# Sample 0's first chunk stores scores for two later chunks, and GpSimd splits its values

## The chip, the cores and the metric

The kernel runs on one core of a Trainium2 chip. The metric is the device time in microseconds (us) of one execution; smaller is better. TensorE multiplies matrices, VectorE and ScalarE work element by element, GpSimd does the same and issues some of the transfers, and SyncE issues transfers only. In the profile they are called PE (with PEld for its weight loads), DVE, ACT, POOL and SP. Each engine takes its own instructions strictly in the order in which they were written; semaphores hold an instruction back until its inputs are there.

## What is computed

Three layers run one after the other on two samples of 3136 tokens with 256 features. The first is an attention without softmax:

```python
scores = scale * np.matmul(z, z.transpose(0, 2, 1))   # scale = 1 / 3136, z is 64 wide
attn = np.maximum(scores, 0.0) ** 2
out = np.matmul(attn, v)
return (u * out).astype(np.float32)
```

Behind it come a mixing layer of rank 32 with a two-layer network of width 1024, and a Fourier mixing layer with normalization and a second network of that width. Only the attention is touched here. Its scores are symmetric: the score of token i against token j is the score of j against i.

## The kernel before

**The attention.** For each sample b the 3136 tokens are taken as queries in seven chunks of 448 (`qc` 0 to 6, `NC` = 7, `CH` = 448). Against one chunk the keys go in 13 steps: twelve pairs of 128 keys (`p` 0 to 11) and a last half pair (`p` = 12). A step has two parts. In `scores`, PE does six matmuls of 448 columns on half of its rows each, so that two run side by side; ACT applies the relu (L735) and the square (L736); then the result is split into a high part `h` (a rounded copy) and a low part `l` (the subtraction, L136). The copy is done by DVE (L742) or, for a "swift" step, by ACT (L133). In `values`, PE multiplies the values `Vt`, which are split in the same way, with `h` and `l`: 24 matmuls for a full pair (L769). Scores are made two steps ahead of the values that use them (`LAG` = 2).

**Kept scores.** Because of the symmetry a step may read its scores instead of making them. In a chunk, `_stored` names the parts of a step's scores that a later chunk will need. For such a step, which the planner calls heavy, `keep` has DVE transpose the scores 32 by 32 into a `turned` tile (L684), and transfers of 112 KB, issued by POOL and SP by turns (L691), write them to `kept_d`. In the later chunk `load_kept` fetches 448 KB through ACT's queue three steps ahead (L665), and `split_kept` makes `h` on ACT and `l` on DVE. No matmul is done, and no relu or square. In sample 0, chunk 0 keeps nothing, so pairs 0 and 1 are always made anew; chunk 4 reads 5 of its 13 steps and chunk 5 reads 6. In sample 1 the same chunks read 7 and 8.

**Order.** `_pairs` sets the order of the 13 steps. Read steps go to fixed places, the half pair to place 6, and the made ones fill the rest, bare ones (nothing to store) first. `ahead(i)` writes out what belongs to step i: the split of the values if this is sample 0's first chunk, the scores, a load of kept scores, the stores of the step before, and pieces of other work: key and query loads, and conversions of weights with their own loads.

**The first chunk.** Chunk 0 of sample 0 also prepares all values of its sample: for each pair a load of 256 KB, a copy to the high part on ACT (L133) and a subtraction for the low part on DVE (L136), both in `parts_v`. The loads go through a few buffers (`vraw`, `stg`, two of each), so SP can issue one only when an older one has been split. POOL has no arithmetic in this chunk: it issues half of the key loads and the next query load, and near the chunk's end it loads constants and makes an identity matrix.

Of the kernel before, what the change touches and what calls it, by code (L numbers as in the profile page):

```python
# [15 lines left out]
ALU = mybir.AluOpType  # L16
# [5 lines left out]
CH = 448  # L22
NC = S // CH
# [20 lines left out]
def _plain(b, p):  # L44
    return (b == 0) & (p < 2)


def _kept(b, qc):

    return [p for p in range(12) if 256 * (p + 1) <= qc * CH and (b or 256 * p >= CH)]  # L50


def _target(p, a):
    return (4 * p + a) // 7, (4 * p + a) % 7 * 64


def _stored(b, qc, p):

    if qc == NC - 1 or not (b or qc):
        return []  # L60
    if p == 12:
        return [(a, NC - 1, 384 + 32 * a) for a in range(2)]
    return [(a, *_target(p, a)) for a in range(4) if _target(p, a)[0] > qc]
# [54 lines left out]
def f(ap):  # L118
    return ap.bitcast(F32)
# [3 lines left out]
def program(ctx, tc, zT, v, uT, U, V, w1a, w2a, w1b, w2b, b49, f64, fd, rep, mask, out):  # L123
    nc = tc.nc
# [7 lines left out]
    def hcopy(o, i):  # L132
        nc.scalar.copy(o, i)  # L133

    def sub(o, a, b):
        tt(out=o, in0=a, in1=b, op=ALU.subtract)  # L136
# [6 lines left out]
    def ctile(tag, dt=F32, **k):  # L143
        return com.tile([128, 2 * CH], dt, tag=tag, name=tag, **k)

    def ptile():
        return ctile("P", bufs=4)

    def c2(t):
        return t.rearrange("p (a n) -> p a n", a=2)  # L150

    def run(gen):
        for _ in gen:
            pass
# [7 lines left out]
    kept_d = {  # L162
        (b, c): dram.tile([c * CH, CH], F32, tag=f"kept{b}{c}", name=f"kept{b}{c}")
        for b in range(NB)
        for c in range(1, NC)
        if _kept(b, c)
    }
    V_d = dram.tile([2 * RANK, S], F32R, tag="Vd", name="Vd")
# [313 lines left out]
    def attention(stack):  # L482
# [11 lines left out]
        def turned_tile():  # L494
            return att.tile([128, 2 * CH], F32, tag="turned", name="turned", bufs=5)
# [97 lines left out]
        def split_v(b, p):  # L593
            run(parts_v(b, p))

        def parts_v(b, p):
            raw, n = vraw.pop((b, p)), 2 if p < 12 else 1
            t = Vt[b, p] = big.tile([128, 2, 2, D], F32R, tag=f"V{p}", name=f"Vt{p}", bufs=1)
            hcopy(t[:, 0:n, 0, :], raw[:, 0:n, :])
            yield  # L600
            sub(t[:, 0:n, 1, :], raw[:, 0:n, :], f(t[:, 0:n, 0, :]))


        def stage():
# [55 lines left out]
        def load_kept(b, qc, p):  # L660
            own = next((k for k in range(2) if loads[k] not in kept), None)
            A = kept[b, qc, p] = ptile() if own is None else turned_tile()
            if own is not None:
                loads[own] = b, qc, p
            nc.scalar.dma_start(out=c2(A), in_=kept_d[b, qc][256 * p : 256 * p + 256].rearrange("(m j) n -> m j n", j=2))  # L665

        def split_kept(b, qc, p):
            A, h, l = kept.pop((b, qc, p)), ctile("h", F32R), ctile("l", F32R)
# [29 lines left out]
        def scores(b, qc, p):  # L698
            ps = psS.tile([128, 2, 512], F32, tag="S", name="psS")
            extra = psO.tile([128, 512], F32, tag="O11", name="psO11") if (b, qc, p) == (0, 0, 0) else None  # L700
            q = Q[b, qc]

            w = CH if p < 12 else CH // 2
            for kk, kq in ((0, 0), (0, 1), (1, 0)):
                for j, r in enumerate(halves):
                    if p == 12:
                        k = KTl[b][r, kk]
                    elif (b, qc) == (0, 0) and p < 2:
                        c = 256 * p + 128 * j
                        k = q[r, kk, c : c + 128]  # L710
                    else:
                        k = KT[b][r, p, kk]
                    o = j * w if p == 12 else 0
                    if extra is None:
                        mm(ps[:, j, 0:w], k, q[r, kq, o : o + w], start=(kk, kq) == (0, 0), stop=kk == 1)  # L715
                    elif (kk, kq) == (0, 0):
                        dst = extra if j else ps[:, j]
                        mm(dst[:, 0:w], first_q[r, c : c + 128], first_q[r, 0:w], start=True, stop=True)
            A, h, l = ptile(), ctile("h", F32R), ctile("l", F32R)

            if (b, qc, p) == (0, 0, 0):
                x, y, B = slice(0, w), slice(w, 2 * w), ptile()
                act(out=A[:, x], in_=ps[:, 0, 0:w], func=AF.Relu, scale=1.0 / S)
                nc.vector.tensor_scalar(
                    out=B[:, y], in0=extra[:, 0:w], scalar1=1.0 / S, scalar2=0.0, op0=ALU.mult, op1=ALU.max
                )
                run(first_v)
                for k, m in ((x, A), (y, B)):
                    act(out=m[:, k], in_=m[:, k], func=AF.Square)
                    nc.vector.tensor_copy(h[:, k], m[:, k])  # L730
                for k, m in ((x, A), (y, B)):
                    sub(l[:, k], m[:, k], f(h[:, k]))
            else:
                x = slice(0, 2 * w)
                act(out=A[:, x].rearrange("p (a n) -> p a n", a=2), in_=ps[:, :, 0:w], func=AF.Relu, scale=1.0 / S)  # L735
                act(out=A[:, x], in_=A[:, x], func=AF.Square)  # L736
                stored = _stored(b, qc, p)
                heavy[0] += bool(stored)
                if turns:
                    keep()  # L740
                swift = stored and heavy[0] % 3 and p != pairs_of[b, qc][-1]
                (hcopy if swift else nc.vector.tensor_copy)(h[:, x], A[:, x])  # L742
                r = slice(0 if p < 12 else 64, 128)
                sub(l[r, x], A[r, x], f(h[r, x]))
                if stored:
                    turns.append((b, qc, p, A))
            prob[b, qc, p] = (h, l)

        acc, heavy = {}, [0]
# [130 lines left out]
        pairs_of = {(b, qc): _pairs(b, qc) for b in range(NB) for qc in range(NC)}  # L880
        order, last_order = pairs_of[0, 0], pairs_of[0, NC - 1]
# [11 lines left out]
        t = att.tile([128, 5, D], F32R, tag="an", name="warm", bufs=1).rearrange("p a n -> p (a n)")  # L893
# [7 lines left out]
        for k in range(20):  # L901
            r, n = halves[k % 2], 128 if k < 8 else 352
# [4 lines left out]
        first_q = qraw[0, 0]  # L907
        split_q(0, 0)
        first_v = parts_v(0, 0)
        next(first_v)  # L910
        split_z(0, 0, slice(2, 3))
        scores(0, 0, 0)

        def ahead(i):
            if i < len(steps):
# [9 lines left out]
                if i + 3 < len(steps) and steps[i + 3][2] in _kept(*steps[i + 3][0:2]):  # L925
                    load_kept(*steps[i + 3])
# [32 lines left out]
        for i in range(-LAG, len(steps)):  # L959
# [3 lines left out]
            if i >= 0:  # L963
                b, qc, p = steps[i]
# [8 lines left out]
                n = i % NP  # L973
# [9 lines left out]
                if (b, qc) == (1, NC - 1):  # L983
                    if n == 2:
                        chunks[0].load()
                        a = c2(turned_tile())
# [316 lines left out]
    with tc.manual_schedule():  # L1303
# [23 lines left out]
        for i in range(nstep + 2):  # L1327
# [3 lines left out]
            early = kp == 7 and i > 2 and chunks[cp].layer == 2  # L1331
# [21 lines left out]
            if i in fetches:  # L1353
                b, k0, k1 = fetches[i]
# [57 lines left out]
```

## Time and profile before

| quantity | value |
|---|---|
| median of 3 runs | 1098.09 us (1093.29 to 1099.11) |
| the profiled execution's own time | 1097.44 us |
| its span, first to last instruction | 1095.7 us |
| PE busy | 1082.7 us, 99% of the span |
| DVE busy | 849.0 us, 77% |
| ACT busy | 622.3 us, 57% |
| POOL busy | 238.0 us, 22% |
| mean granted clock of PE | 0.997 of full speed |

Matmuls are pipelined and their ends are modelled, so PE's busy share says that it seldom stood still, not that it was at its peak. The places where it did stand still are found in the time line, by gaps in front of its instructions. The attention takes the first 513 us, in fourteen chunks of 32 to 39 us each; their borders can be read from the `gate` of each chunk (L801), which is the first work on a chunk's finished sums. A stretch from gate to gate is one chunk's pace.

### The profile page before, as it was taken

How to read it: one execution, taken by the hardware profiler on the slowest of the kernel's cores; microseconds unless marked ns; L12 is line 12 of the kernel's file. 1: busy time of each engine (PE TensorE's matmuls, PEld its weight loads, DVE VectorE, ACT ScalarE, POOL GpSimd, SP SyncE). 2: the span in 40 equal slices, each digit the busy share in tenths (PEclk: the TensorE clock that was granted, in tenths of full speed). 3: DMA queues.
4: the chain of work that ended last, by engine and by line, in shares of the span. 5: the costliest groups of instructions: out<-in, count | busy, mean ns of one | idle time of the engine just before them, and what ended most of it. 6: DMA issues, size and time to landing. Idle time of an engine off the chain costs nothing.

```text
span 1095.7 us, 21312 instructions
## 1 busy us (share of the span) xinstructions
PE 1082.7 (99%) x7926; PEld 1010.2 (92%) x7926; DVE 849.0 (77%) x1571; ACT 622.3 (57%) x1094; POOL 238.0 (22%) x394
## 2 busy tenths in 40 slices
PE   9999999989999999999999999999999999999998
PEld 8999999979999999899899999999999999999997
DVE  7898888778999988666667777676688888778863
ACT  7888777747898777553334444334345454445431
POOL 2143332110534232121111121111141111011110
PEclk9999999999999999999999999999999999999999
DMA  6366668674767677985813454221153231121210
GB/s 176 94 168 169 178 175 239 188 240 131 202 186 197 202 214 214 287 239 156 244 45 112 123 177 110 73 78 44 44 130 110 71 89 46 35 60 51 59 43 34
DMA packets 182248, 148.81 MB, mean 136 GB/s; under 512 B 115734, under 2 KB 156474, under 8 KB 182144
## 3 DMA queue, kind: packets, MB, share of 16 engines
q1 hardware_dynamic: 152416, 77.84, 26.4%
q0 software_dynamic: 21296, 43.21, 14.1%
q10 hardware_dynamic: 8432, 26.40, 8.0%
q8 instruction: 62, 1.02, 0.4%
q14 instruction: 42, 0.34, 0.1%
HBM read 88.61 MB, written 58.75 MB: 134 GB/s over the span
## 4 chain that ended last, share of the span: by engine, by line
PE 79%; DVE 7%; DMA 6%; ACT 4%; issue 2%; SPq 0%; POOL 0%; DVEq 0%; ACTq 0%
PE psO L769 24%; PE psH L427 8%; PE psH L429 8%; PE psC L454 8%; PE psH L428 8%; PE psC L452 8%; PE psC L453 8%; PE psS L715 4%; DVE l L136 2%; DMA kept<-turned 2%; DVE turned L684 1%; ACT P L736 1%; ACT P L735 1%; DMA stg<-in_v 1%; ACT h L133 1%
## 5 line engine op out<-in xcount | busy, mean ns | idle before, releaser
L769 PE MATMUL psO<-h,Vt 64*128 64x448 f32 x2744 | 335.2, 362 | 4.5 <-DVE h L742 3.9
L769 PEld LDWEIGHTS psO<-h,Vt 64*128 64x128 f32 x2744 | 279.5, 185 | 21.4 <-DVE h L742 7.3
L432 ACT ACTIVATE Hh<-psH 128x448 fp32r<-128x448 f32 x224 | 121.5, 543 | 244.2 <-PE psH L429 240.6
L433 DVE SCALAR_TENSOR_TENSOR Hl<-psH,Hh 128x448 fp32r<-128x448 f32 x224 | 138.0, 618 | 109.3 <-ACT Hh L432 107.3
L136 DVE TENSOR_TENSOR l<-P,h 128x896 fp32r<-128x896 f32 (+2 forms) x185 | 167.2, 911 | 57.7 <-ACT h L133 50.2
L769 PE MATMUL psO<-l,Vt 64*128 64x448 f32 x1372 | 194.8, 362 | 3.2 <-DVE l L136 3.0
L427 PE MATMUL psH<-h,w 128*128 128x448 f32 x448 | 164.9, 368 | 0.0
L429 PE MATMUL psH<-h,w 128*128 128x448 f32 x448 | 162.4, 363 | 0.0
L454 PE MATMUL psC<-Hh,w 128*128 128x448 f32 x448 | 162.4, 362 | 0.0
L428 PE MATMUL psH<-l,w 128*128 128x448 f32 x448 | 162.2, 362 | 0.0
L453 PE MATMUL psC<-Hl,w 128*128 128x448 f32 x448 | 162.1, 362 | 0.0
L452 PE MATMUL psC<-Hh,w 128*128 128x448 f32 x448 | 162.0, 362 | 0.0
L769 PEld LDWEIGHTS psO<-l,Vt 64*128 64x128 f32 x1372 | 148.4, 185 | 13.1 <-DVE l L136 7.3
L691 POOL DMA_DIRECT2D kept<-turned x134 | 87.4, 656 | 176.9 <-DVE turned L684 142.4
L735 ACT ACTIVATE P<-psS 128x896 f32<-128x896 f32 (+1 forms) x124 | 107.9, 871 | 28.6 <-PE psS L715 25.2
L736 ACT ACTIVATE P<-P 128x896 f32<-128x896 f32 (+1 forms) x124 | 113.1, 912 | 3.9
L133 ACT CAST h<-P 128x448 fp32r<-128x448 f32 (+1 forms) x108 | 77.0, 724 | 55.0 <-DVE P L318 39.6
L427 PEld LDWEIGHTS psH<-h,w 128*128 128x128 f32 x448 | 84.1, 188 | 6.3 <-issue 0.3
L453 PEld LDWEIGHTS psC<-Hl,w 128*128 128x128 f32 x448 | 84.0, 187 | 6.0
L428 PEld LDWEIGHTS psH<-l,w 128*128 128x128 f32 x448 | 84.2, 188 | 5.8
L715 PE MATMUL psS<-Q,KT 64*128 64x448 f32 x654 | 89.3, 362 | 0.0
L452 PEld LDWEIGHTS psC<-Hh,w 128*128 128x128 f32 x448 | 83.9, 187 | 5.7 <-issue 0.2
(299 smaller groups left out, 1379.8 us busy)
## 6 DMA issues: line engine op xcount, KB each, us to landing
turned<-kept ACTq DMA_DIRECT2D x52, 448.0 KB, 4.1
kept<-turned POOLq DMA_DIRECT2D x123, 112.0 KB, 3.7
kept<-turned SPq DMA_DIRECT2D x118, 112.0 KB, 3.7
uT<-in_uT SPq DMA_DIRECT2D x14, 448.0 KB, 4.4
out<-P SPq DMA_DIRECT2D x27, 224.0 KB, 1.9
aTd<-turned POOLq DMA_DIRECT2D x13, 448.0 KB, 5.9
scr<-wst SPq DMA_DIRECT2D x16, 256.0 KB, 2.0
vraw<-in_v SPq DMA_DIRECT2D x13, 256.0 KB, 4.8
```

Source lines behind the costliest of these rows:

```text
L136: tt(out=o, in0=a, in1=b, op=ALU.subtract)
L427: mm(ps[:, 0:CH], wh, self.h[:, a], start=a == 0, stop=False)
L428: mm(ps[:, 0:CH], wh, self.l[:, a], start=False, stop=False)
L429: mm(ps[:, 0:CH], wl, self.h[:, a], start=False, stop=a == 1)
L432: act(out=h, in_=ps[:, 0:CH], func=AF.Relu)
L433: stt(out=l, in0=ps[:, 0:CH], scalar=0.0, in1=f(h), op0=ALU.max, op1=ALU.subtract)
L452: mm(dst, wh, h, start=k == 0, stop=False)
L453: mm(dst, wh, l, start=False, stop=False)
L454: mm(dst, wl, h, start=False, stop=k == 7)
L715: mm(ps[:, j, 0:w], k, q[r, kq, o : o + w], start=(kk, kq) == (0, 0), stop=kk == 1)
L736: act(out=A[:, x], in_=A[:, x], func=AF.Square)
L769: mm(o[fa][i][:, 0:CH], vt[r, j, k, fa * 128 : fa * 128 + 128], x[r, j * CH : j * CH + CH], start=n0 == 0 and fa not in [t[1][0] for t in ...
```

## The change

Three things are changed. First, `_kept` lets chunks 4 and 5 of sample 0 read pairs 0 and 1 as well, and `_stored` has chunk 0 store what they need: four quarters each of pairs 7, 8 and 9 and two of pair 10. The pairs 0 and 1 of sample 0 lie in another layout of keys, so `load_kept` reads those in two blocks. Second, in `parts_v` GpSimd makes both parts of the values in sample 0, except for the first pair. Third, of the four steps of chunk 0 that now store, those of pairs 7 and 9 have their `h` made by ACT; the counter `heavy`, which chooses swift steps later on, leaves chunk 0 out.

```diff
 def _kept(b, qc):
-    return [p for p in range(12) if 256 * (p + 1) <= qc * CH and (b or 256 * p >= CH)]
+    return [p for p in range(12) if 256 * (p + 1) <= qc * CH and (b or 256 * p >= CH or qc in (4, 5))]
...
-    if qc == NC - 1 or not (b or qc):
+    if qc == NC - 1:
         return []
+    if not (b or qc):
+        return [(a, *_target(p, a)) for a in range(4) if p < 12 and _target(p, a)[0] in (4, 5)]
...
             t = Vt[b, p] = big.tile([128, 2, 2, D], F32R, tag=f"V{p}", name=f"Vt{p}", bufs=1)
-            hcopy(t[:, 0:n, 0, :], raw[:, 0:n, :])
-            yield
-            sub(t[:, 0:n, 1, :], raw[:, 0:n, :], f(t[:, 0:n, 0, :]))
+            early = b == 0 and p != order[0]
+            (nc.gpsimd.tensor_copy if early else hcopy)(t[:, 0:n, 0, :], raw[:, 0:n, :])
+            yield
+            (nc.gpsimd if early else nc.vector).tensor_tensor(
+                out=t[:, 0:n, 1, :], in0=raw[:, 0:n, :], in1=f(t[:, 0:n, 0, :]), op=ALU.subtract
+            )
...
-            nc.scalar.dma_start(out=c2(A), in_=kept_d[b, qc][256 * p : 256 * p + 256].rearrange("(m j) n -> m j n", j=2))
+            how = "(j m) n -> m j n" if _plain(b, p) else "(m j) n -> m j n"
+            nc.scalar.dma_start(out=c2(A), in_=kept_d[b, qc][256 * p : 256 * p + 256].rearrange(how, j=2))
...
                 stored = _stored(b, qc, p)
-                heavy[0] += bool(stored)
+                heavy[0] += bool(stored) and b + qc > 0
                 if turns:
                     keep()
-                swift = stored and heavy[0] % 3 and p != pairs_of[b, qc][-1]
+                swift = stored and (heavy[0] % 3 if b + qc else p % 2) and p != pairs_of[b, qc][-1]
```

What this does to the order is seen at three places. A row has the line, the operation, the tile written and the tiles read, its shape, and how often it comes in a row; numbers behind a name tell buffers apart. The lines of the changed file stand a few higher than in the file before.

The first place is POOL's queue in chunk 0 of sample 0, behind the load of the first keys. Before:

```order
L512 DMA turned_181<-in_zT 64x64
L510 DMA turned_224<-in_zT 64x768
L510 DMA turned_324<-in_zT 64x768
L565 DMA qraw_331<-in_zT 64x448 x2
L508 DMA turned_418<-in_zT 64x2x128 x2
masks.py:197 MEMSET ident_90 128x128
```

And now:

```order
L514 DMA turned_181<-in_zT 64x64
L602 CAST Vt1_186<-vraw_149 128x2x256
L604 ISA
L604 TENSOR_TENSOR Vt1_186<-vraw_149,Vt1_186 128x2x256
L602 CAST Vt2_207<-vraw_154 128x2x256
L604 TENSOR_TENSOR Vt2_207<-vraw_154,Vt2_207 128x2x256
L512 DMA turned_224<-in_zT 64x768
L602 CAST Vt3_287<-stg_184 128x2x256
L604 TENSOR_TENSOR Vt3_287<-stg_184,Vt3_287 128x2x256
L602 CAST Vt4_307<-stg_205 128x2x256
L604 TENSOR_TENSOR Vt4_307<-stg_205,Vt4_307 128x2x256
L512 DMA turned_324<-in_zT 64x768
```

The splits of the values stand in front of the key loads that POOL issued one after the other before.

The second place is DVE's queue around the ninth and tenth steps of chunk 0 (pairs 7 and 8). Before:

```order
L136 TENSOR_TENSOR Vt7_492<-stg_375,Vt7_492 128x2x256
L742 CAST h_503<-P_502 128x896
L136 TENSOR_TENSOR l_504<-P_502,h_503 128x896
L136 TENSOR_TENSOR KT_0_161<-turned_418,KT_0_161 128x2x128
L136 TENSOR_TENSOR Q_515<-qraw_331,Q_515 128x448
L136 TENSOR_TENSOR Vt8_524<-vraw_423,Vt8_524 128x2x256
L742 CAST h_535<-P_534 128x896
L136 TENSOR_TENSOR l_536<-P_534,h_535 128x896
```

And now:

```order
L138 TENSOR_TENSOR l_504<-P_502,h_503 128x896
L138 TENSOR_TENSOR KT_0_161<-turned_418,KT_0_161 128x2x128
L138 TENSOR_TENSOR Q_515<-qraw_331,Q_515 128x448
L690 STREAM_TRANSPOSE turned_539<-P_502 128x14x2x32
L748 CAST h_535<-P_534 128x896
L138 TENSOR_TENSOR l_536<-P_534,h_535 128x896
L690 STREAM_TRANSPOSE turned_584<-P_534 128x14x2x32
L138 TENSOR_TENSOR l_581<-P_579,h_580 128x896
```

The subtractions for the values are gone from DVE, and a transpose stands in front of the next step's `h`.

The third place is ACT's queue at the start of chunk 5 of sample 0, behind the gate's copies from `psO`. Before:

```order
L133 COPY turned_3021<-psO10_2510 128x448
L735 ACTIVATE P_3035<-psS_3028 128x896
L736 ACTIVATE P_3035<-P_3035 128x896
L133 CAST KT_1_2771<-vraw_2883 128x2x128
L735 ACTIVATE P_3051<-psS_3044 128x896
L736 ACTIVATE P_3051<-P_3051 128x896
L665 DMA turned_3058<-kept05_79 128x896
L216 ACTIVATE stg_2829<-stg_2829,maskc_92 128x256
L217 ACTIVATE stg_2829<-stg_2829,maskc_92 128x256
L133 CAST h_3099<-turned_2964 128x896
```

And now:

```order
L135 CAST h_3054<-turned_2925 128x896
L671 DMA turned_3058<-kept05_79 128x896
L218 ACTIVATE stg_2835<-stg_2835,maskc_92 128x256
L219 ACTIVATE stg_2835<-stg_2835,maskc_92 128x256
L135 CAST h_3099<-turned_2972 128x896
L135 CAST KT_1_2777<-vraw_2978 128x2x128
L135 CAST h_3140<-P_3050 128x896
L671 DMA turned_3144<-kept05_79 128x896
L135 CAST w_2953<-stg_2835 128x2x128
L135 CAST h_3178<-turned_3058 128x896
```

Four read steps (`h_3054`, `h_3099`, `h_3140`, `h_3178`) now follow one another, with the weights' copy `w` between the third and the fourth; before, made steps stood between the read ones.

## Rows read from the trace of the kernel before

**Rows 1.** The page: busy time by engine, and the chain that ended last.
```profile
PE 1082.7 (99%) x7926; PEld 1010.2 (92%) x7926; DVE 849.0 (77%) x1571; ACT 622.3 (57%) x1094; POOL 238.0 (22%) x394
PE 79%; DVE 7%; DMA 6%; ACT 4%; issue 2%; SPq 0%; POOL 0%; DVEq 0%; ACTq 0%
```
**Rows 2.** Windows from gate to gate: sample 0's chunks 0, 4, 5, 6; sample 1's 4, 5.
```profile
core 0: us, PE busy (x) PEld busy (x) DVE busy (x) ACT busy (x) POOL busy (x), PEclk, DMA share, GB/s
8.08:43.83 35.75, 35.49 (x354) 32.35 (x354) 31.91 (x49) 31.38 (x46) 4.51 (x8) 1.00 0.46 125
...
153.60:189.78 36.18, 35.53 (x357) 34.61 (x355) 29.90 (x49) 28.07 (x42) 11.39 (x18) 1.00 0.82 230
189.78:224.98 35.20, 33.92 (x332) 30.78 (x330) 29.12 (x49) 24.25 (x38) 5.97 (x9) 1.00 0.66 183
224.98:263.70 38.72, 35.66 (x325) 33.04 (x323) 26.58 (x36) 22.42 (x32) 3.25 (x5) 0.91 0.70 213
...
411.34:443.76 32.42, 32.17 (x325) 30.81 (x323) 26.65 (x38) 22.63 (x31) 8.29 (x13) 1.00 0.80 225
443.76:477.73 33.97, 33.72 (x347) 30.90 (x345) 21.91 (x26) 18.78 (x23) 5.93 (x9) 1.00 0.86 254
```
**Rows 3.** Chain of waits in chunk 0: start, length, what; one step.
```profile
23.31 0.60 PE psS L715 x6
23.91 2.40 PE psO L769 x24
```
**Rows 4.** Groups by form in chunk 0 (8.08 to 43.83 us): busy, mean ns, idle before.
```profile
L136 DVE TENSOR_TENSOR l<-P,h 128x896 fp32r<-128x896 f32 x12 | 13.1, 1092 | 1.1
...
L742 DVE CAST h<-P 128x896 fp32r<-128x896 f32 x12 | 7.5, 623 | 2.6 <-ACT P L736 2.5
L136 DVE TENSOR_TENSOR Vt<-stg,Vt 128x512 fp32r<-128x512 f32 x6 | 4.1, 684 | 0.0
L133 ACT CAST Vt<-stg 128x512 fp32r<-128x512 f32 x6 | 3.7, 609 | 0.0
...
L136 DVE TENSOR_TENSOR KT<-turned,KT 128x384 fp32r<-128x384 f32 x3 | 1.7, 553 | 0.0
...
L136 DVE TENSOR_TENSOR Q<-qraw,Q 128x448 fp32r<-128x448 f32 x1 | 0.6, 619 | 0.0
```
**Rows 5.** Groups by form on DVE, 0 to 270 us: the transpose of a stored step.
```profile
L684 DVE STREAM_TRANSPOSE turned<-P 128x896 f32<-128x896 f32 x28 | 30.8, 1100 | 0.2
```
**Rows 6.** Groups by form on POOL, whole span: a write of 512 columns, a transfer's issue.
```profile
L691 POOL DMA_DIRECT2D kept<-turned x134 | 87.4, 656 | 176.9 <-DVE turned L684 142.4 <-DVE turned L681 23.6 <-DVE stg L214 3.6
...
L1063 POOL MEMSET nh<- 32x512 f32 x3 | 1.6, 519 | 0.0
```
**Rows 7.** Time lines of POOL and DVE where both work: start, length, instruction.
```profile
8.94 0.69 POOL masks.py:199 TENSOR_SCALAR_AFFINE_SELECT ident<-ident 128x128 f32<-128x128 f32 x1
...
9.39 0.78 DVE L136 TENSOR_TENSOR Vt<-vraw,Vt 128x512 fp32r<-128x512 f32 x1
...
529.39 0.28 DVE L214 TENSOR_SCALAR Tl<-Tl 128x256 int32<-128x256 int32 x1
...
548.17 0.67 POOL L1063 MEMSET nl<- 32x512 f32 x1
...
548.29 0.69 DVE L214 TENSOR_SCALAR Tl<-Tl 128x256 int32<-128x256 int32 x1
```
**Rows 8.** ACT in chunk 5 by form: a read step's copy, the weights' copy.
```profile
L133 ACT CAST h<-turned 128x896 fp32r<-128x896 f32 x6 | 5.6, 931 | 0.0
...
L133 ACT CAST w<-stg 128x256 fp32r<-128x256 f32 x3 | 1.2, 407 | 6.8 <-DMA stg<-in_w1a 3.9 <-DVE stg L221 2.9
```
**Rows 9.** Chunk 6 of sample 0: PE's time line, then the window around its gap.
```profile
244.02 1.11 PE L769 MATMUL psO<-h,Vt 64*128 64x448 f32 x3 [3.03 <-DVE h L742]
...
240.00:250.00 10.00, 6.97 (x41) 6.08 (x41) 6.32 (x9) 6.82 (x11) 0.00 (x0) 0.67 0.75 236
```

## Prediction

> **What bounds the kernel now.** I read the page first: PE is busy 99% of the span and carries 79% of the chain that ended last [rows 1]. So work taken from PE is time won, and work put on other engines costs only where PE comes to wait for it. Next I cut the attention from gate to gate [rows 2]. A made step costs PE 0.60 us of scores and every full step 2.40 us of values [rows 3], so a chunk with k read steps cannot be shorter than 12 x 2.40 + 0.60 for the half pair's values, plus 12 x 0.60 + 0.30 for its scores, minus 0.60 k: 36.9 - 0.6 k. Chunk 4 (k = 5) should take 33.9 and takes 36.18; chunk 5 (k = 6) should take 33.3 and takes 35.20; chunk 6 (k = 8) should take 32.1 and takes 38.72 [rows 2]. Chunk 0 shows no such loss: PE is busy for 35.49 of 35.75 us, with DVE at 31.91 and ACT at 31.38 beside it [rows 2]. The reader is to see two things there: in chunk 0 PE sets the pace already, and DVE and ACT stand only 3.8 and 4.4 us below it.
>
> **What the change removes.** Four scoring steps, two in chunk 4 and two in chunk 5. On PE that is 4 x 0.60 = 2.4 us [rows 3]; 24 score matmuls less stand in PE's order. This lies on the path. On DVE a step that is read spares one conversion, 0.62 us [rows 4], and on ACT two passes for one copy of 0.93 us [rows 8]; both engines are below the pace in these chunks (29.90 and 28.07 of 36.18 us [rows 2]), so I count this at nothing, except that it may soften the chunks' short waits, by less than 1 us. In chunk 0, 11 full and one half split of the values leave DVE (11.5 x 0.684 = 7.9 us) and ACT (11.5 x 0.609 = 7.0 us) [rows 4]. Since PE did not wait there, this wins nothing by itself.
>
> **What it adds in chunk 0.** Four transposes on DVE, 4 x 1.10 = 4.4 us [rows 5]. Two conversions go from DVE to ACT (1.2 us off DVE). DVE's own sum thus falls by 7.9 + 1.2 - 4.4 = 4.7 us. Fourteen writes of 112 KB fall on transfer engines that are busy 0.46 of this stretch [rows 2]: hidden. Their issue costs POOL 7 x 0.656 = 4.6 us [rows 6].
>
> POOL gets the splits. No row shows GpSimd copying or subtracting such a tile. The nearest is a write of 512 columns without any input, 0.519 us [rows 6]; a copy should not be cheaper. DVE's subtraction of this size takes 0.684 us [rows 4], so 0.52 + 0.68 = 1.2 us is the low end for a split. The high end comes from the one POOL operation that reads: 0.69 us for 128 columns [rows 7]; four times that, 2.76 us, and 0.52 give 3.3 us. I take the sub at two passes of the memset, one for each input, 1.04 us, and the split at 1.56 us, because the memset has the right number of columns while the 0.69 us includes a wait, as I argue next. So 11.5 x 1.56 = 18 us of arithmetic, beside about 15 transfers at 0.656 = 10 us, in a stretch of 35.75: POOL is not the bound by its own sum. The Trainium skill ("GPSIMD Engine Reference", Performance versus the Vector engine) gives 4497 ns for an add of 2048 columns; a quarter is 1.12 us (an estimate), and with it the split would be 1.64 us and the sum below 0.9 us longer.
>
> **The collision.** The rows show POOL and DVE holding each other up. DVE's L214 takes 0.28 us alone and 0.69 us when a POOL memset runs beside it; it ends where the memset ends [rows 7]. At 9.39 us a DVE subtraction of 512 columns takes 0.78 us against a mean of 0.684 [rows 4, 7], in the only place where POOL was reading SBUF, and that POOL operation needed 0.69 us for 128 columns. I read this as one resource that one of the two holds for a whole instruction. That a conversion collides is firm; that a subtraction with two inputs does rests on one event of 0.1 us. The Trainium skill ("SBUF — State Buffer", Who interferes with whom) states it for both: a conversion in the two-port mode collides with any GpSimd operation, a DVE instruction with two inputs in SBUF with one that reads. By that rule, the trace agrees; its page "Perfetto Trace Analysis" warns that moving work between these two may not help for this reason.
>
> If both collide, their times add up. DVE keeps in chunk 0: 11 subtractions x 1.092 = 12.0, nine conversions x 0.623 = 5.6, key and query subtractions 1.7 + 0.6 = 2.3; together 19.9 us [rows 4]. The transposes have one input; I let POOL run beside them. POOL's 18 us make it 37.9 us. All this has to happen between PE's first values and the last values' start, some 33 us of the 35.75. So chunk 0 grows by **5 us**. With a split of 1.2 us the same sum gives 33.7 and +1; with 3.3 us POOL alone needs 38 + 10 = 48 us and chunk 0 grows by 15. Without any collision it grows by nothing.
>
> POOL's order adds a smaller risk: the key loads L512 and the constants now stand behind splits, and ACT's copy of the keys, then its relu, queue behind a late key load. With the split at 1.56 the loads still come in time; this is in the high end.
>
> **What it adds in chunks 4 and 5.** Four loads of 448 KB, 1.8 MB. Sample 1's chunks 4 and 5 already read seven and eight steps with the same places and take 32.42 and 33.97 us [rows 2], 0.3 below and 1.9 above the bound, though with transfers at 0.80 and 0.86. Sample 0 has keys of the next sample and weights to load besides. In chunk 5 ACT already stood for 3.9 us at the weights' copy for its transfer [rows 8]; this cost PE little, because made steps followed. Now four read steps follow one another there and that copy stands in front of the fourth. Each read step needs 448 KB within 2.4 us, 187 KB per us, near the 183 to 254 GB/s that these chunks reach in all [rows 2]. I price lateness there at +1 us, between -1 (the waits soften) and +6 (below).
>
> **Sum.** Against the profiled execution's own 1097.4 us (0.65 below the median, which I do not correct for): -2.4 + 5 + 1 = +3.6, that is **1101.0 us**.
>
> **The rivals.**
> - *No collision of subtractions, POOL hidden.* Then chunk 0 stays as it is and the four steps are won: 1097.4 - 2.4 = 1095.0, down to 1093 if the waits in chunks 4 and 5 soften. For it: the weak single event in [rows 7], POOL's own sum fits. Against it: conversions collide all the same.
> - *Chunk 5 stalls as chunk 6 does (slower).* In chunk 6 of sample 0 the same four read places meet loads of values; PE stood for 3.03 us and the granted clock was 0.67 in those 10 us, which is between the two levels of 1.2 and 2.4 GHz [rows 9]. That idle time and a third of 10 us at the lower clock make some 6 us. If the weights' or the keys' transfer in chunk 5 comes more than about 3 us late, PE's lead of one to two steps is used up and the same follows: 1097.4 - 2.4 + 5 + 6 = 1106; without the collision, 1101.
> - *GpSimd near the high price.* Chunk 0 grows by 10 to 15 us: 1105 to 1110.
> - *The edit does less than it says.* The four steps are gone from PE's order, so this leaves only the case that PE waits for the kept scores instead: 1097.4 + 5, or 1102.
>
> **How the numbers follow.** Collision with hidden transfers 0.55 (1101, from 1097 to 1105 with the split between 1.2 and 1.9 us), no collision 0.25 (1095), chunk 5's stall 0.11, GpSimd's high price 0.06, waits for kept scores 0.03. The two ends: 1093 is the no-collision case with softer waits; 1108 takes in the stall and part of the high price. Less than 2 in 10 is left outside. About 0.5%, 5.5 us around 1098.1, is what a measurement of this kernel can tell from no change. Faster than 1092.6: 0.08, the best part of the second case. Slower than 1103.6: the stall with collision (0.08), the high price (0.06) and the upper part of the first case (0.14), 0.28. The rest, 0.64, is the same.
>
> **What would show it.** In the changed profile the gate-to-gate stretch of chunk 0 tells most: about 41 us means collision, 36 none. There DVE's conversions should take longer than 0.62 us and its subtractions than 1.09, with PE's gaps released by `h`, `l` or `Vt`. GpSimd's split itself should show 1.2 to 1.9 us. Chunks 4 and 5 should shrink by 1.2 us each; a gap of PE in chunk 5 behind ACT's copy of weights or keys would show the stall. If chunk 0 stays at 36 us while DVE's operations keep their lengths, the collision was wrong, and with it the sign of my sum.

## Result

| | before | changed |
|---|---|---|
| median of 8 runs | 1098.32 us (1093.29 to 1099.19) | 1104.05 us (1102.07 to 1107.15) |
| ratio to before | | 1.0065, 95% interval 1.0045 to 1.0085 |
| span of the profiled execution | 1095.7 us | 1101.7 us |

The changed kernel is slower by 0.65%, some 6 to 7 us. The predicted time was 1101.0 us, in a range of 1093 to 1108. The measured one lies inside, 3 us above the point and just past the bound of 0.5% that the prediction set for a change that can be told from none.

The gate-to-gate windows of the changed kernel, beside [rows 2]: chunks 0, 4, 5 and 6 of sample 0 (stretch, length, busy time of each engine with its instructions, granted clock, share of the transfer engines, GB/s).

```profile
core 0: us, PE busy (x) PEld busy (x) DVE busy (x) ACT busy (x) POOL busy (x), PEclk, DMA share, GB/s
8.00:52.41 44.41, 37.74 (x348) 33.00 (x346) 43.32 (x40) 28.03 (x37) 40.75 (x44) 1.00 0.49 138
163.52:198.92 35.40, 34.68 (x337) 30.83 (x333) 28.46 (x47) 26.53 (x40) 11.41 (x18) 1.00 0.92 257
198.92:233.18 34.26, 32.93 (x320) 29.63 (x321) 27.47 (x47) 22.86 (x36) 5.69 (x9) 1.00 0.71 204
233.18:268.32 35.14, 33.02 (x324) 30.47 (x322) 26.48 (x35) 22.33 (x32) 3.52 (x6) 1.00 0.75 232
```

Chunk 0 reaches its first gate at 52.41 instead of 43.83 us. PE, which was busy for 35.49 of 35.75 us in [rows 2], now stands in it for 6.7 us. DVE has nine instructions less and is busy for 43.32 instead of 31.91 us; POOL works 40.75 of 44.41 us. Chunk 4 is 0.8 and chunk 5 0.9 us shorter. Chunk 6, which the change does not touch, is 3.6 us shorter; what that means is taken up below.

The groups by form in chunk 0 of the changed kernel, beside [rows 4] and [rows 5] (count, busy, mean ns, idle before):

```profile
L138 DVE TENSOR_TENSOR l<-P,h 128x896 fp32r<-128x896 f32 x12 | 18.0, 1504 | 0.9
L748 DVE CAST h<-P 128x896 fp32r<-128x896 f32 x10 | 10.7, 1072 | 0.0
L604 POOL TENSOR_TENSOR Vt<-stg,Vt 128x512 fp32r<-128x512 f32 x6 | 9.6, 1603 | 0.5
...
L602 POOL CAST Vt<-stg 128x512 fp32r<-128x512 f32 x6 | 5.7, 943 | 0.0
...
L690 DVE STREAM_TRANSPOSE turned<-P 128x896 f32<-128x896 f32 x4 | 4.4, 1103 | 0.0
L138 DVE TENSOR_TENSOR KT<-turned,KT 128x384 fp32r<-128x384 f32 x3 | 2.6, 853 | 0.0
```

The same subtraction takes DVE 1.50 us on average instead of 1.09, the conversion 1.07 instead of 0.62, the key subtraction 0.85 instead of 0.55. Only the transpose keeps its 1.10 us. It reads one tensor, as the conversion does, but needs 1.10 us for the 896 columns that an unhindered conversion does in 0.62 us [rows 4, 5].

What GpSimd's split costs by itself is seen at the one place of this kernel where it met a transpose. POOL's and then DVE's time line there (start, length, instruction):

```profile
40.91 0.62 POOL L602 CAST Vt<-stg 128x512 fp32r<-128x512 f32 x1
41.62 1.30 POOL L604 TENSOR_TENSOR Vt<-stg,Vt 128x512 fp32r<-128x512 f32 x1
...
40.95 1.10 DVE L690 STREAM_TRANSPOSE turned<-P 128x896 f32<-128x896 f32 x1
41.97 1.89 DVE L138 TENSOR_TENSOR l<-P,h 128x896 fp32r<-128x896 f32 x1
```

0.62 us for the copy, 1.30 for the subtraction: 1.92 us. The transpose runs beside them unhurt. (In the kernels e3 and e8 below, two transposes each run beside a subtraction of GpSimd and take 1.10 to 1.11 us as well.) The DVE subtraction that is entered at 41.97 takes 1.89 us instead of 1.09: it ends 0.94 us after GpSimd's subtraction does, so most of its work came behind it. PE's time line shows who pays (in brackets the gap before, and what ended it):

```profile
32.53 1.87 PE L775 MATMUL psO<-h,Vt 64*128 64x448 f32 x16 [1.33 <-DVE h L748]
39.98 1.88 PE L775 MATMUL psO<-h,Vt 64*128 64x448 f32 x16 [1.17 <-DVE h L748]
48.65 0.68 PE L775 MATMUL psO<-h,Vt 64*128 64x448 f32 x4 [1.19 <-POOL Vt L602]
50.73 0.67 PE L775 MATMUL psO<-h,Vt 64*128 64x448 f32 x4 [1.40 <-POOL Vt L604]
```

### The profile page after: what moved, and what is told of

It reads as the page before. It is cut to its first block, busy times and chain, and to the rows that moved or that the text cites. A ratio compares the mean times of both kernels' runs of the same rounds, so it can differ in the third digit from the quotient of the medians.

```text
span 1101.7 us, 21301 instructions
## 1 busy us (share of the span) xinstructions
PE 1082.3 (98%) x7902; PEld 1004.5 (91%) x7902; DVE 857.0 (78%) x1557; ACT 615.5 (56%) x1080; POOL 271.6 (25%) x425
## 4 chain that ended last, share of the span: by engine, by line
PE 78%; DVE 7%; DMA 5%; ACT 5%; issue 3%; POOL 1%; SPq 1%; ACTq 0%; DVEq 0%; POOLq 0%
PE psO L775 21%; PE psH L429 8%; PE psH L431 8%; PE psC L456 8%; PE psH L430 8%; PE psC L454 8%; PE psC L455 8%; PE psS L721 3%; DMA aNd<-turned 2%; DVE l L138 2%; ACT P L742 2%; ACT P L741 2%; ACT h L135 1%; DVE turned L690 1%; DVE h L748 1%
## 5 line engine op out<-in xcount | busy, mean ns | idle before, releaser
L775 PEld LDWEIGHTS psO<-h,Vt 64*128 64x128 f32 x2744 | 273.8, 184 | 32.1 <-DVE h L748 5.1
L138 DVE TENSOR_TENSOR l<-P,h 128x896 fp32r<-128x896 f32 (+2 forms) x182 | 169.8, 940 | 55.7 <-ACT h L135 49.1
L775 PE MATMUL psO<-l,Vt 64*128 64x448 f32 x1372 | 191.8, 361 | 3.6 <-DVE l L138 3.1
L775 PEld LDWEIGHTS psO<-l,Vt 64*128 64x128 f32 x1372 | 144.6, 184 | 14.8 <-DVE l L138 8.9
L697 POOL DMA_DIRECT2D kept<-turned x141 | 92.1, 657 | 183.7 <-DVE turned L690 142.1
L741 ACT ACTIVATE P<-psS 128x896 f32<-128x896 f32 (+1 forms) x120 | 104.3, 869 | 38.3 <-PE psS L721 35.4
L742 ACT ACTIVATE P<-P 128x896 f32<-128x896 f32 (+1 forms) x120 | 109.3, 911 | 3.8
L135 ACT CAST h<-P 128x448 fp32r<-128x448 f32 (+1 forms) x111 | 80.2, 733 | 55.6 <-DVE P L320 39.2
L429 PEld LDWEIGHTS psH<-h,w 128*128 128x128 f32 x448 | 84.1, 188 | 6.4 <-issue 0.3
L431 PEld LDWEIGHTS psH<-h,w 128*128 128x128 f32 x448 | 84.1, 188 | 5.4
```

Source lines behind the costliest of these rows:

```text
L429: mm(ps[:, 0:CH], wh, self.h[:, a], start=a == 0, stop=False)
L431: mm(ps[:, 0:CH], wl, self.h[:, a], start=False, stop=a == 1)
L775: mm(o[fa][i][:, 0:CH], vt[r, j, k, fa * 128 : fa * 128 + 128], x[r, j * CH : j * CH + CH], start=n0 == 0 and fa not in [t[1][0] for t in ...
```

## Experiments

Where the stretches are compared, these are the gates read from each run's time line. "0+1" is the time from 8 us to the end of chunk 1, "4+5" the sum of those two chunks of sample 0, "6" its chunk 6. The time is the median of the timed runs, or that of the profiled run where it is the only one. The ratio compares with runs of the kernel before that were timed beside it, whose medians in these series were 1096.7 to 1097.0 us, so a time of this column is not to be set against the 1098.3 of its first row.

The two profiles of the kernel before differ by 0.8 us at the first gate, 0.9 us in chunks 4 and 5 and 2.6 us in chunk 6. Every other row is one profile, so a difference of 1 us between two rows shows nothing by itself.

| kernel | first gate | 0+1 | 4+5 | 6 | time, us | ratio to before |
|---|---|---|---|---|---|---|
| before | 43.8 | 73.6 | 71.4 | 38.7 | 1098.3 | |
| before, once more (e6) | 44.6 | 74.4 | 70.5 | 36.1 | 1095.8 | one run |
| changed | 52.4 | 82.9 | 69.7 | 35.1 | 1104.1 | 1.0065 |
| scores only (e1) | 46.9 | 78.2 | 69.7 | 36.3 | 1098.0 | 1.0008 |
| split only (e2) | 52.5 | 82.3 | 71.7 | 36.7 | 1105.0 | 1.0073 |
| copy on ACT (e3) | 48.6 | 79.1 | 70.9 | 34.8 | 1100.4 | one run |
| subtraction on DVE (e4) | 49.1 | 80.8 | 69.5 | 35.0 | 1101.8 | one run |
| before with memsets (e5) | 44.8 | 74.6 | 71.6 | 34.6 | 1095.0 | one run |
| constants later (e7) | 51.8 | 82.9 | 71.7 | 39.2 | 1107.9 | one run |
| four subtractions (e8) | 45.7 | 75.9 | 70.0 | 34.3 | 1097.6 | 1.0007 |
| scores only, no transpose (e9) | 44.8 | 75.0 | 70.6 | 34.4 | 1096.8 | 1.0000 |
| another order (e10) | 47.7 | 76.9 | 71.6 | 34.3 | 1098.4 | 1.0013 |

### The two halves of the change, each alone

The scores part alone, in the changed kernel:

```diff
-            early = b == 0 and p != order[0]
-            (nc.gpsimd.tensor_copy if early else hcopy)(t[:, 0:n, 0, :], raw[:, 0:n, :])
+            hcopy(t[:, 0:n, 0, :], raw[:, 0:n, :])
             yield
-            (nc.gpsimd if early else nc.vector).tensor_tensor(
-                out=t[:, 0:n, 1, :], in0=raw[:, 0:n, :], in1=f(t[:, 0:n, 0, :]), op=ALU.subtract
-            )
+            sub(t[:, 0:n, 1, :], raw[:, 0:n, :], f(t[:, 0:n, 0, :]))
```

> The changed kernel with the values of sample 0 split on ACT and DVE as before; chunk 0 still stores for chunks 4 and 5, which read two steps more each. Theory (GpSimd's splits collide with DVE's subtractions and conversions and cost chunk 0 its 8.6 us): chunk 0 ends its first gate near 44 to 46 us instead of 52.4, DVE's subtractions of 896 columns take 1.09 us again, and the run is 1094 to 1098 us. Rival 1 (the four transposes and the stores of chunk 0 cost it): chunk 0 still ends above 48 us and the run stays above 1100. Rival 2 (the four read steps bring nothing because of their loads): chunks 4 and 5 take as long as in the kernel before, 36.2 and 35.2 us, and the run is 1098 or more.

Measured: ratio 1.0008 (0.9995 to 1.002), the first gate at 46.9 us, 0.9 later than I had expected, and DVE's long subtractions at 1.09 us again. So most of chunk 0's growth is GpSimd's. But not all of it: chunks 0 and 1 still took 78.2 us, 4.2 more than the mean of the two profiles of before, which neither the theory nor my sum had. PE's time line at the end of chunk 0, and the windows around it, show where:

```profile
44.01 1.55 PE L772 MATMUL psO<-h,Vt 64*128 64x448 f32 x8 [1.61 <-DVE h L745]
...
40.00:44.00 4.00, 2.37 (x22) 1.53 (x18) 3.85 (x5) 3.16 (x4) 3.92 (x8) 1.00 0.72 180
44.00:48.00 4.00, 3.99 (x24) 3.38 (x26) 3.34 (x4) 0.53 (x1) 0.22 (x1) 0.57 0.34 90
```

PE waits 1.61 us for the `h` that DVE makes behind the last of four transposes. The eight matmuls after it take 1.55 us, where eight took 0.97 us just before: behind the gap the granted clock was at its lower level, 0.50 of full speed, for 3.4 us, and 0.57 in the mean of 44 to 48 us. By the mean, 4 x 0.43 = 1.7 us of the 4.2 are the clock's (an estimate). Chunks 4 and 5 took 1.3 us less than the mean of before, little more than the 0.9 us between the two profiles of before; this half came out level. By this run alone, the rival that the read steps bring nothing is not excluded.

The other half alone, in the kernel before: the same lines of `parts_v` the other way round, nothing else.

> The kernel before with one part of the change alone: GpSimd splits the values of sample 0's first chunk. Theory (the splits collide): the first gate comes at 51 to 53 us instead of 43.8, as in the changed kernel, chunks 4 and 5 stay at 36.2 and 35.2 us, and the run is 1102 to 1108 us. Rival 1 (the transposes cost it): the first gate comes below 46 us and the run is within 3 us of the kernel before. Side question, chunk 6 of sample 0 (38.7 us before, 35.2 after): if it is short here as well, the later start of the chunks shortened it; if it is long, the extra read steps did.

Measured: 1105.0 us, ratio 1.0073 (1.0049 to 1.0097), first gate at 52.5 us, chunks 4 and 5 as before. GpSimd's split alone costs as much as the whole change. At first sight the two halves do not add up: 8.2 us (split) and 4.2 us (stores) in chunks 0 and 1, but 8.9 together. The clock can account for it. In this kernel too it fell, behind a gap of 2.28 us, and again for 3.4 us (columns as in the first windows above):

```profile
41.00:45.00 4.00, 4.00 (x26) 4.00 (x28) 3.79 (x5) 0.00 (x0) 3.92 (x7) 0.57 0.26 81
```

In the changed kernel it stayed at 1.00 in both chunks. Without 1.7 us each, the split costs 6.5 and the stores 2.5 us, 9.0 together (an estimate), which agrees with 8.9 within the scatter.

### Which instructions collide

Only the high part goes back to ACT:

```diff
-            (nc.gpsimd.tensor_copy if early else hcopy)(t[:, 0:n, 0, :], raw[:, 0:n, :])
+            hcopy(t[:, 0:n, 0, :], raw[:, 0:n, :])
```

> The changed kernel with the high part of the values copied on ACT as before; GpSimd makes the subtraction only, 1.3 to 1.6 us for each of 12 pairs. Theory (GpSimd's reads collide with DVE's two-input subtractions and with its conversions): DVE needs 19.9 us of the shared resource and GpSimd 15 to 18, so chunk 0 still grows, to a first gate of 46 to 50 us, and several of DVE's 896-column subtractions take over 1.3 us. Rival (only DVE's conversions collide): all of those subtractions take 1.09 us and only conversions are longer than 0.62. Rival (POOL's queue is the bound): the first gate comes about 12 times 0.9 us earlier than 52.4 or not later than the kernel before, 43.8.

Measured: the first gate at 48.6 us, in the range of the theory and 3.8 us before that of the changed kernel. DVE's groups in chunk 0 of this kernel, and PE's longest gap there:

```profile
L138 DVE TENSOR_TENSOR l<-P,h 128x896 fp32r<-128x896 f32 x12 | 18.4, 1532 | 1.2 <-ACT h L135 0.3
...
L748 DVE CAST h<-P 128x896 fp32r<-128x896 f32 x10 | 8.0, 804 | 0.1
...
46.90 0.68 PE L775 MATMUL psO<-h,Vt 64*128 64x448 f32 x4 [2.35 <-POOL Vt L604]
```

The subtractions are stretched as much as in the changed kernel, to 1.53 us, the conversions less. The rival that only conversions collide falls. The time is weaker evidence: 2.35 us of it is a wait for the last split, whose copy ACT had ready at 40.7 us while POOL was issuing writes and the constants until 45.6. So here POOL's queue took part.

Only the low part goes back to DVE:

```diff
-            (nc.gpsimd if early else nc.vector).tensor_tensor(
+            nc.vector.tensor_tensor(
```

> The changed kernel with only the copy of the values on GpSimd; the subtraction for their low part is back on DVE. GpSimd then reads one input, 0.62 us for 512 columns when nothing is in its way. Theory (every GpSimd instruction that reads holds back DVE's two-input subtractions, for as long as it runs): some of the 896-column subtractions take up to 0.7 us more than 1.09, the mean 1.2 to 1.4; GpSimd's 12 x 0.62 = 7 us and DVE's 19.9 + 7.9 us make 35, so the first gate comes at 46 to 50 us. Rival (only a GpSimd instruction with two inputs collides with a subtraction): all of them keep 1.09 us.

Measured: the first gate at 49.1 us, as expected, but the long subtractions kept 1.09 us on average, against the number that I had put down. The order explains it: in this run GpSimd's copies fell on other instructions, or came while a long subtraction was under way and were then stretched themselves (the copy at 29.57 takes 1.01 us). DVE's key subtractions, also of two inputs, went from 0.55 us [rows 4] to 0.83. The time line shows two copies meeting DVE's 512-column subtractions, which need 0.68 us elsewhere (the group, then POOL's rows, then DVE's):

```profile
L138 DVE TENSOR_TENSOR KT<-turned,KT 128x384 fp32r<-128x384 f32 x3 | 2.5, 831 | 0.0
...
29.57 1.01 POOL L602 CAST Vt<-vraw 128x512 fp32r<-128x512 f32 x1 [2.87 <-DMA vraw<-in_v]
...
36.21 0.63 POOL L602 CAST Vt<-stg 128x512 fp32r<-128x512 f32 x1
...
30.02 1.10 DVE L604 TENSOR_TENSOR Vt<-stg,Vt 128x512 fp32r<-128x512 f32 x1
...
36.24 1.15 DVE L604 TENSOR_TENSOR Vt<-vraw,Vt 128x512 fp32r<-128x512 f32 x1
```

The second is plain: GpSimd starts 0.03 us ahead, and DVE is late by 0.47 us. So a GpSimd instruction with one input holds DVE's subtraction too; the rival falls on these events, not on the mean that I named. (Here too the clock was at 0.50 for 3.4 us, behind a gap of 2.85 us; about 1.7 of the 80.8 us are due to it.)

The counter-test lets GpSimd write only. In the kernel before, ahead of each split of chunk 0:

```diff
+            if b == 0 and p != order[0]:
+                if not scratch:
+                    scratch.append(att.tile([128, 5, D], F32, tag="an", name="scratch", bufs=1).rearrange("p a n -> p (a n)"))
+                for cols in (640, 1280):
+                    nc.gpsimd.memset(scratch[0][:, 0:cols], 0.0)
             hcopy(t[:, 0:n, 0, :], raw[:, 0:n, :])
```

> The kernel before with two memsets on GpSimd, of 640 and 1280 columns, about 1.9 us together, ahead of each of the 12 splits in chunk 0; they write to a tile that nobody uses, read nothing, and wait for nobody, so they run in the first 30 us. Theory (a conversion on DVE collides with anything that GpSimd does, a subtraction only with a GpSimd instruction that reads): conversions of 896 columns take up to 1.3 us longer than 0.62 while the memsets run, subtractions keep 1.09 us (within 0.05). Rival (any two instructions of the two collide): subtractions are stretched too. Rival (the subtractions in the changed kernel were stretched by late inputs, not by GpSimd): neither is stretched. Time: 0 to 5 us above the kernel before.

The groups from 4 to 32 us, in which the memsets ran:

```profile
L605 POOL MEMSET scratch<- 128x1280 f32 x11 | 14.5, 1315 | 0.6
...
L136 DVE TENSOR_TENSOR l<-P,h 128x896 fp32r<-128x896 f32 x7 | 7.6, 1093 | 0.6
L605 POOL MEMSET scratch<- 128x640 f32 x11 | 7.4, 672 | 1.5 <-issue 1.1
L749 DVE CAST h<-P 128x896 fp32r<-128x896 f32 x7 | 5.9, 847 | 0.6 <-ACT P L743 0.6
```

GpSimd is busy for 22 of 28 us, and DVE's subtractions take 1.093 us, against 1.092 before, while its conversions go from 0.62 to 0.85 us. This tells all three apart: late inputs are no cause, "any two collide" is no rule, and what a subtraction shares with GpSimd is used by reads alone. The first gate came at 44.8 us, where the two profiles of before have 43.8 and 44.6, so GpSimd's time by itself costs next to nothing.

### POOL's own queue

In the changed kernel, the constants are loaded in chunk 1:

```diff
-                if (b, qc, p) == (0, 0, 11):
+                if (b, qc, p) == (0, 1, 4):
```

> The changed kernel with the load of the constants, five transfers on GpSimd's queue and the identity matrix, moved from the end of chunk 0 to the fifth step of chunk 1. In the changed kernel they stand in front of the last split of values, and PE stood for 1.2 and 1.4 us at that split. If POOL's queue costs these 2.6 us, the first gate comes at 49.5 to 50.5 us instead of 52.4. If the shared resource alone sets the pace, it comes within 1 us of 52.4, since PE then waits for DVE's h or l instead.

Measured: the first gate at 51.8 us, 0.6 earlier, which is inside the scatter. PE's two waits for POOL's `Vt` are gone and others stand in their place:

```profile
47.49 0.68 PE L775 MATMUL psO<-l,Vt 64*128 64x448 f32 x4 [0.51 <-DVE l L138]
49.11 1.07 PE L775 MATMUL psO<-h,Vt 64*128 64x448 f32 x8 [0.94 <-DVE h L748]
```

So in the changed kernel the constants in POOL's queue did not set the pace; PE had only named the last of two late things. The other work in that queue was not moved. The run as a whole took 1107.9 us, with chunk 6 at 39.2 us, the longest of all profiles; that is the scatter of the next section.

### Chunk 6 of sample 0

> The kernel before, profiled once more, to see how far chunk 6 of sample 0 differs from one execution to the next. If its 38.7 us belong to the kernel, they come again within 0.5 us, with the low clock in 240 to 250 us; if the low clock there is chance, the chunk comes out at 34.5 to 37 us as in the four kernels of the first series. All chunks ahead of it should repeat within 0.5 us, the first gate at 43.8 us.

The kernel before, profiled again, had chunk 6 at 36.1 instead of 38.7 us, with PE's longest gap at 1.42 us instead of 3.03. The chunks ahead of it repeated less well than I had expected: the first gate came at 44.6 instead of 43.8 us. The kernels between them span 34.3 to 39.2 us without any relation to the change: e5 and e9 have it short, the changed kernel with another place for constants has it longest. Where PE stood for over 3 us, the mean clock of the 10 us around it was 0.66 to 0.67; read in steps of 1 us it was 0.50 for some 6.8 us, before as in the kernel with the constants later. Beside the window in [rows 9]:

```profile
240.00:250.00 10.00, 8.52 (x65) 7.15 (x65) 8.11 (x12) 8.87 (x14) 0.00 (x0) 0.83 0.86 277
```

is that window in the second profile, with 3.4 us at 0.50. In chunk 6 the clock fell for 3.4 us in e1, e2 and e6, behind gaps of 1.4 to 2.0 us, and not at all in the changed kernel, with a gap of 2.0 us. So the 3.6 us that chunk 6 seemed to win lie within what two executions of one kernel differ by, and nothing ties them to the change. Chunk 6 may be much of the spread of 6 us among the runs of one kernel; that was not shown. What makes its gap long or short was not settled.

### Versions that might keep the gain

Four subtractions only, where the transposes are:

```diff
-            early = b == 0 and p != order[0]
-            (nc.gpsimd.tensor_copy if early else hcopy)(t[:, 0:n, 0, :], raw[:, 0:n, :])
+            early = b == 0 and 7 <= p <= 10
+            hcopy(t[:, 0:n, 0, :], raw[:, 0:n, :])
```

> The changed kernel with GpSimd making only the subtraction for the values of pairs 7 to 10, whose steps are near those with a transpose; all other splits are on ACT and DVE as before. Theory: DVE is relieved of 4 x 0.68 us where the transposes add 4 x 1.10, and a transpose can run beside GpSimd, so in these steps DVE's 1.7 us and GpSimd's 1.3 us of the shared resource fit in PE's 3.0 us; the first gate comes at 44 to 46 us, 1 to 3 us ahead of the kernel that has scores only (46.9), and the run is 0 to 3 us below the kernel before. Rival (any GpSimd subtraction in chunk 0 costs more than it relieves): the first gate comes at 47 us or later and the run is level with the kernel before or above it.

Measured: first gate at 45.7 us, 1.2 earlier than with scores only, and a run level with before (1.0007, 0.9993 to 1.0021). The gate is where it was expected, but it does not show the mechanism: the clock stayed at 1.00 here, and in the scores-only kernel its fall alone cost about 1.3 us up to the first gate. Without it the two gates are level (an estimate).

How much there is to win is seen by leaving out the transposes in the scores-only kernel:

```diff
-            t = turned_tile()
+            t = turned_tile() if b + qc else A
             rows = slice(qc * CH, qc * CH + CH)
-            if p == 12:
+            if b + qc == 0:
+                n = 64
+            elif p == 12:
```

> The kernel with the scores part alone (values split on ACT and DVE), but chunk 0 of sample 0 stores its scores as they are, without the four transposes on DVE; the part that is left out is that transposition, so two steps each of chunks 4 and 5 read scores in the wrong order. All transfers stay. Theory (the four transposes, 4 x 1.10 us on a DVE that is full at the end of chunk 0, cost chunks 0 and 1 their 4 us in the kernel with scores alone): the first gate comes at 44 to 45 us instead of 46.9, PE has no gap over 0.6 us there, and the run is 1 to 3 us below the kernel before, which is what the four read steps are worth. Rival (ACT's two conversions or the stores cost it): the first gate stays above 46 us and the run level with the kernel before.

Measured: the first gate at 44.8 us, level with the second profile of before, and PE's longest gap in chunk 0 from 8 us on is 0.37 us. Chunks 0 and 1 take 3.3 us less than with scores only; about 1.7 of these are the clock, which stayed at 1.00 here, and 1.6 are left for the four transposes. But the run is level with before, 1.0000 (0.9987 to 1.0013), so the expected 1 to 3 us did not come, though no transpose is paid for here. At the end of that interval the whole run wins 1.4 us; chunks 0 and 1 still lost 0.9 us against the mean of before, so the four read steps are worth 2.3 us at the very most.

The last version changes the order of chunk 0, on top of the four subtractions:

```diff
-        return plain
+        return plain if b else [*range(6), 12, 7, 6, 8, 9, 11, 10]
...
-            early = b == 0 and 7 <= p <= 10
+            early = b == 0 and 6 <= p <= 9
```

> A version that might beat both: as the kernel with four subtractions on GpSimd, but with the steps of chunk 0 in another order (pairs 7, 6, 8, 9, 11, 10 at its end, so that the four storing steps don't follow one another) and GpSimd making the subtraction for pairs 6 to 9. If the transposes hurt because they come in a row, the first gate comes about 1 us earlier than 45.7 and the run is 0.5 to 2 us below the kernel before. If DVE's whole sum in chunk 0 is what counts, it stays level with the kernel before.

Measured: first gate at 47.7 us, 2.0 later than with the plain order, and 1.0013 (1.0002 to 1.0024), slightly slower than the kernel before. Neither of the two expectations came, and since the order and GpSimd's pairs were changed at once, it is not known which of them costs it. No version here beats the kernel before.

## Why the prediction was right

The direction and the cause came as forecast, and the point lies 3 us below the measured time, which is inside the range. The odds are a nearer thing: by its own bounds the prediction gave 0.64 to "the same" and 0.28 to "slower than 1103.6", and 1104.05 us lies 0.5 us over that bound, with an interval that reaches to both sides of it.

**What bounds the kernel.** Right: chunk 0 has PE as its bound. Of the 8.7 us by which it grew, 6.4 are gaps of PE in front of matmuls that wait for `h` or `Vt`; the other 2.2 are longer busy time of PE for about as many matmuls, at a clock of 1.00. Their ends are modelled, so these were not traced.

**The collision.** Right, and it was the decision that gave the sum its sign. What the prediction called firm was less so: the event at L214 in [rows 7] is an operation on integers with one scalar, and not a conversion. That conversions do the same was carried over, and it was e5 that showed it (0.62 to 0.85 us beside memsets). In the changed kernel both halves hold: 0.62 to 1.07 us for conversions, 1.09 to 1.50 for subtractions. The low price of 0.69 us for 128 columns in [rows 7] was read rightly as a wait: the same operation takes 0.29 us at 44.41 us in the changed kernel. The Trainium skill's rule ("SBUF — State Buffer", Who interferes with whom) fits what these runs show: the memsets of e5 hold conversions and spare subtractions, a copy with one input holds a subtraction (e4), and the transpose is spared.

**Chunk 0's +5 us was too small.** One price was too low: GpSimd's split takes 1.92 us unhindered, where I put 1.56 with two passes of a memset for the subtraction; it takes 1.30. The same sum with 11.5 x 1.92 = 22 us and DVE's 19.9 us makes 42 us in 33, +9 us, and 8.9 us were measured for chunks 0 and 1 against the mean of both profiles of before. The prediction's own range for a split of up to 1.9 us ends at 1105, close to the time that came out. But that the sum hits so well is partly luck. For the split alone (e2), where two conversions more stay on DVE, it gives +10 us, and 8.2 were measured, about 6.5 without the clock. For e3 (19.9 + 15 us in 33) and e4 (19.9 + 7.9 + 7.1 us in 33) it gives +2 us, and 5.1 and 6.8 were measured, where e4 has about 1.7 from the clock and both carry the stores. So adding the two engines' times gives the sign, and the size to within some 4 us. The parts measured in the profiles, +8.9 and -0.9 us, also make a little more than the timed runs, which grew by 6 to 7 us; the rest was not traced.

**The transposes counted at nothing.** This term was wrong. With the splits still on DVE (e1) the stores cost 4.2 us in chunks 0 and 1, 2.5 without the clock, although DVE's sum was 3.8 us below PE's pace over the whole chunk. 1.6 us of that go with the transposes (e9). My reason, that the sum of DVE's work falls, left out that all four come in the last steps. In the changed kernel the stores cost about as much: it took 82.9 us against 82.3 for the split alone, 80.6 without the clock. By this estimate the sum at 1.92 us puts too much on the split and nothing on the stores, and the two errors nearly cancel.

**Chunks 4 and 5: -2.4 + 1.** Eight kernels with the read steps took 70.4 us on average for both chunks (69.5 to 71.7), the four without 71.3 (70.5 to 71.7): a gain of 0.9 us, give or take about as much. That is in keeping with -1.4 and does not confirm it. The cause was not what I named. A copy of weights on ACT did wait in the changed kernel, 4.6 us, which the profile puts down to the load of `uT`, and PE had no gap from it. What came up was a new wait at the gate of chunk 4, in all eight profiles with read steps and in none of the four without:

```profile
199.59 1.08 PE L775 MATMUL psO<-h,Vt 64*128 64x448 f32 x7 [0.63 <-DVE turned L807]
```

PE waits there for DVE to read the sums of the chunk before. Seven of the eight, though not the changed kernel, also have one to three waits of 0.2 to 0.6 us for an `h` that ACT makes; of the four without, only e2 has one. PE's idle time in the two chunks rose from 1.8 to 2.8 us on average, which is 1.0 of the 1.5 us that are missing; the rest was not traced.

**The rivals.** "No collision" fell. Chunk 5's stall did not come. GpSimd's high price did not come: 1.92 us lies between 1.56 and 3.3. In chunks 4 and 5 of the changed kernel no gap of PE was put down to a load of kept scores.

## What to carry to other kernels

Before giving GpSimd a share of VectorE's elementwise work, add up their times as for one engine, for VectorE's subtractions of two tensors and its conversions, and compare that sum with the pace of the stage. In these runs it told the sign, and the size to within some 4 us; a free GpSimd was no free capacity. The 32 by 32 transpose could run beside it. A step spared on the bounding engine can be worth less than its length: four steps of 0.6 us gave about 0.9 us here, too little to be told from the scatter. And before two profiles are compared, read the granted clock in both: a stretch at the lower level cost 1.7 us in three of these kernels, more than some of the effects looked for.

## What the hardware showed

GpSimd needs 0.62 us to copy and 1.30 us to subtract 128 x 512 values, against 0.61 us on ACT and 0.68 us on DVE [rows 4]. A GpSimd instruction that only writes did not slow a two-input subtraction of DVE by as much as 0.01 us, even when it ran almost 80% of the time (e5). The granted clock of PE was 1.00 nearly throughout. Behind some gaps it was at its lower level, 0.50 of full speed (1.2 of 2.4 GHz): for about 6.8 us at gaps of 3.0 and 3.6 us, and for 3.4 us, which cost PE 1.7 us of work, behind gaps between 1.4 us (e6) and 2.9 us (e4). It stayed at 1.00 behind a gap of 2.0 us in the changed kernel and one of 2.35 us in e3. So the length of a gap alone does not decide it, and what does was not tested.
